# Five shared rows of wo: four of them moved from the partitions of DMA engine 3 to those of engines 2 and 4

## The chip, the cores and the metric

The kernel runs on one core of one Trainium2 chip. The metric is the device time of one launch in microseconds (us), as a median over several runs. Lower is better.

## What is computed

One decode step: an attention block over a cache, mixed by a gate with a small dense block. Cut to what matters:

```python
g = sigmoid((x * gate_w).sum(-1))                    # x: 1 x 1 x 512
q = (x @ wq) in 32 heads of 128                      # wq: 512 x 4096
scores = q . k_cache * 128 ** -0.5                   # 32 heads, 4096 keys of 128
o = softmax(scores) . v_cache                        # 32 heads, 4096 values of 128
a = o.reshape(4096) @ wo                             # wo: 4096 x 512
b = relu(x @ w1 + b1) ** 2 @ w2 + b2                 # w1: 512 x 1376, w2: 1376 x 512
out = g * a + (1 - g) * b                            # 1 x 1 x 512, all bf16
```

The two caches are 32 MB each, so the launch has 78.3 MB to read and very little arithmetic for each byte.

## The kernel before, in words

**Loads.** SP's queue issues, in a fixed order, four parts of `wq`, then `K0` to `K6`, then `V0`, `K7`, `V1`, `K8` and so on up to `V31` (`LAG` is 7). Each of these is one transfer of 128 partitions by 8 KB into a ring of 8 buffers (`Kt`, `Vt`). A load of K waits until VectorE and TensorE are done with the buffer (`s_sd`, `s_t`), one of V until its product is done (`s_pv`). `w1` and a first part of `w2` come after `K15` and `K17`; the rest of `w2` (`w2b`, `w2a`) and the last eight heads' part of `wo` (`wob_sb`, in `Kt`'s buffer 0) come at the very end, behind `V31`.

**Work on a head.** VectorE multiplies half of the keys by the head's q (L635), TensorE transposes the other half (L436) and multiplies (L447); ScalarE takes the exponentials; TensorE multiplies by V (`pv`, L472). Behind the last head come the sums with `wo` (L516, L535, L544), `w2` (L553), a transpose and the store.

**wo of the first 24 heads.** These 96 x 128 rows of `wo` are seen as 96 long rows of 32 KB (`woa_v`), and each long row goes into one partition of the tile `W`, where `wq` stood until its last use. Only 96 of the 128 partitions are needed, and the kernel chooses them:

[...]
- `RUNS`: 76 long rows, issued by POOL's queue at L327 (with small dummy transfers at L324 that turn the queue's round robin to the wanted engine), so that each row is carried by the engine that serves its partition. `FIRST`: 15 long rows in five transfers by SP's queue at L279, three rows each, on engines 0, 1 and 2. Counted from the two lists, engine 3 carries no whole row; engines 4, 5, 6 and 9 to 14 carry 5 each; engines 1 and 2 carry 7; engines 0, 7, 8 and 15 carry 8.
- `REST`: the last five long rows, in the list that the change touches. Each is cut into 16 parts of 2 KB, and each part into 1984 and 64 bytes, so that all 16 engines carry one sixteenth of it (L285). All of these parts land in one partition. They are issued with `V20`/`K27`, `V21`/`K28`, up to `V24`/`K31`, one row each time, and stand behind that K in the queue.

**Use of the rows.** `STRIPS` lists all the placements. POOL builds a selection matrix `selA` from it (L342, one instruction for each entry), by which `spread_a` puts each head's output on the partition that holds its row; partitions without a row get zeros. TensorE multiplies the first 23 columns (`out_a`, L516), VectorE the last nine (`part_y`, L682 and L685), and both wait for all of the rows (`s_wp`, `s_wr`).

Of the kernel before, what the change touches and what calls it, by code (L numbers as in the profile page):

```python
# [5 lines left out]
def bass_gated_mix__gqa_block_cached__dense_activation_squared_relu__decode_kernel(  # L6
# [57 lines left out]
            (SEAM, 7, 2, 3, 1), (WRAP, 15, 2, 3, 1)]  # L64
    FIRST = [(INNER, 0, 3, 0, 1), (INNER, 0, 3, 1, 1), (INNER, 0, 3, 2, 1), (INNER, 0, 3, 3, 1),
             (OUTER, 0, 3, 0, 1)]
    REST = [12, 13, 14, 15, 44]
    HF = 20

    def place(kind, e, k, r, m):  # L70
        if kind == INNER:
            return 32 + 4 * e + r, 4 // m, k * m
        if kind == OUTER:
            return (4 * e if e < 8 else 64 + 4 * e) + r, 4, k
        if kind == SEAM:
            return 28 + r, 68, k
        return r, 124, k
# [9 lines left out]
    def strips():  # L87
        q = 0
        for run in RUNS + FIRST:
            yield (*place(*run), q)  # L90
            q += place(*run)[2]
        for n, p in enumerate(REST):
            yield p, 1, 1, q + n
# [12 lines left out]
    with ctx:  # L106
# [147 lines left out]
        def _(eng):  # L254
# [16 lines left out]
            for h in range(NH):  # L271
# [5 lines left out]
                if HF <= h < HF + len(FIRST):  # L277
                    p, st, k, q = STRIPS[len(RUNS) + h - HF]
                    eng.dma_start(W[p:p + st * (k - 1) + 1:st, :], woa_v[q:q + k, :],  # L279
                                  max_dma_last_dim=8192).then_inc(s_wr, 16)  # L280
                if HF <= h < HF + len(REST):
                    p, _, _, q = STRIPS[len(RUNS) + len(FIRST) + h - HF]
# [113 lines left out]
        def _(eng):  # L396
# [111 lines left out]
            def out_a(n):  # L508
                if n == 0:
                    eng.wait_ge(s_ac, 2)  # L510
                    for q in s_wp:
                        eng.wait_ge(q, 16)
                    eng.wait_ge(s_wr, 16 * (len(FIRST) + 2 * len(REST)))
                for t in range(4 * n, min(4 * n + 4, TD)):
# [87 lines left out]
        def _(eng):  # L602
# [85 lines left out]
            for i in range(NH + LAG):  # L688
# [17 lines left out]
                if i == 33:  # L706
# [4 lines left out]
                    for q in s_wp:  # L711
                        eng.wait_ge(q, 16)
                    eng.wait_ge(s_wr, 16 * (len(FIRST) + 2 * len(REST)))
                    eng.wait_ge(s_y2, 1)
# [39 lines left out]
```

## Time and profile before

| | |
|---|---|
| median of 3 runs | 202.44 us (202.22 to 202.49) |
| profiled execution, its own time | 202.31 us |
| its span, first to last instruction | 200.5 us |
| DMA moved in the span | 78.76 MB, mean 393 GB/s |
| VectorE, TensorE, ScalarE busy | 69%, 67%, 40% of the span |
| K loads: 32 of 1024 KB, issue to landing | median 26.7 us |
| V loads: 32 of 1024 KB, issue to landing | median 27.4 us |

The page cuts the span into 40 slices of 5 us and gives the busy share in tenths. Beside what the page sums up, the trace holds each DMA packet (queue, start, duration, size) and each moment at which a load's semaphore was raised. A K or V load raises its semaphore 16 times, once for each DMA engine; the engine is not named, but the 16 moments of a load in order of time show how far apart the engines stand. The load is usable at the sixteenth.

### The profile page before, as it was taken

Reading aid. Unit: us, or ns where it says so; the run is one execution under the profiler, and the core shown is the slowest. Engines: PE = TensorE matmul, PEld = TensorE weight load, DVE = VectorE, ACT = ScalarE, POOL = GpSimd, SP = SyncE. Lnnn points to the kernel's source line nnn. Section 1 sums busy time; section 2 is a strip of 40 time slices with the busy share of each in tenths; the row PEclk is TensorE's granted clock in tenths of the full one; section 3 lists DMA queues with packets and bytes.
Section 4 is the critical chain, followed back from the end, with each engine's and each line's share of the span. In section 5 each row is a group of like instructions: output and inputs, shape, how many; then the busy total and the mean of one; then the engine's idle time right before and its main releaser. Section 6 shows DMA issues by size and latency. Waiting matters only on the chain.

```text
span 200.5 us, 6579 instructions
## 1 busy us (share of the span) xinstructions
PE 134.5 (67%) x2405; PEld 119.6 (60%) x2405; DVE 138.9 (69%) x1151; ACT 79.5 (40%) x148; POOL 30.6 (15%) x56
## 2 busy tenths in 40 slices
PE   0138657598986867646297763469997753598485
PEld 0106636387776667446276763459987653588484
DVE  0307999999998687447477774476699985577701
ACT  2105847376473336413147331433274330632000
POOL 2000000000000000000019930000398740000000
PEclk9999966655555555555555555555555555555555
DMA  6999999999999999999999999999999999999940
GB/s 236 426 425 425 418 420 422 415 418 425 409 415 425 420 414 411 419 419 419 418 425 417 412 418 407 410 407 415 413 406 401 402 393 415 374 425 415 372 173 10
DMA packets 12962, 78.76 MB, mean 393 GB/s; under 512 B 2658, under 2 KB 2836, under 8 KB 3861
## 3 DMA queue, kind: packets, MB, share of 16 engines
q1 hardware_dynamic: 11459, 75.83, 92.5%
q0 software_dynamic: 1456, 2.50, 3.3%
q8 instruction: 19, 0.31, 0.6%
q14 instruction: 14, 0.11, 0.2%
q10 hardware_dynamic: 14, 0.01, 0.0%
HBM read 78.32 MB, written 0.00 MB: 391 GB/s over the span
## 4 chain that ended last, share of the span: by engine, by line
DMA 59%; DVE 16%; SPq 12%; PE 9%; issue 2%; ACT 0%; DVEq 0%
DMA Kt<-in_A_k_cache_dram 41%; DVE Kt L635 14%; DMA Vt<-in_A_v_cache_dram 13%; DMA W<-in_A_wq_dram 5%; SPq L262 4%; SPq L267 3%; SPq L285 3%; PE KP L436 2%; PE pQ L414 2%; PE pQ L472 1%; DVE S L635 1%; SPq L279 1%; PE pO L472 1%; PE pX L544 1%; PE pS L447 1%
## 5 line engine op out<-in xcount | busy, mean ns | idle before, releaser
L635 DVE CUSTOM_DVE_ANT_0 Kt<-Kt,qb 128x128 bf16<-128x128 bf16 x512 | 113.4, 290 | 30.2 <-DMA Kt<-in_A_k_cache_dram 30.2
L370 ACT ACTIVATE kT<-KP 128x1024 bf16<-128x1024 bf16 x64 | 61.9, 1021 | 74.6 <-PE KP L436 74.6
L436 PE MATMUL KP<-ident,Kt 128*128 128x128 bf16 x512 | 57.1, 300 | 38.5 <-DMA Kt<-in_A_k_cache_dram 38.5
L436 PEld LDWEIGHTS KP<-ident,Kt 128*128 128x128 bf16 x512 | 49.6, 140 | 41.2 <-DMA Kt<-in_A_k_cache_dram 40.1
L635 DVE DVE_READ_ACCUMULATOR2_ANT S<- 128x1 f32 x512 | 41.3, 81 | 0.0
L447 PE MATMUL pS<-qcol,kT 128*128 128x1 bf16 x512 | 19.3, 167 | 8.3 <-DVE S L641 8.3
L447 PEld LDWEIGHTS pS<-qcol,kT 128*128 128x128 bf16 x512 | 19.0, 108 | 9.7 <-DVE S L641 9.7
L324 POOL DMA_DIRECT2D xb<-in_B_w_dram x9 | 5.4, 599 | 102.7 <-PE pQ L414 102.7
L414 PE MATMUL pQ<-W,xb 128*128 128x512 bf16 x32 | 15.0, 624 | 6.5 <-DMA W<-in_A_wq_dram 6.5
L472 PEld LDWEIGHTS pO<-E,Vt 128*128 128x128 bf16 x512 | 15.6, 105 | 1.2 <-issue 0.8
L472 PE MATMUL pO<-E,Vt 128*128 128x1 bf16 x512 | 16.2, 166 | 0.0
L342 POOL TENSOR_SCALAR_AFFINE_SELECT w_sb<-w_sb 24x36 bf16<-24x36 bf16 (+6 forms) x23 | 12.1, 527 | 3.7 <-POOL w_sb L342 0.5
L362 ACT ACTIVATE qb<-pQ 128x512 bf16<-128x512 f32 x8 | 4.7, 592 | 15.4 <-PE pQ L414 15.4
L414 PEld LDWEIGHTS pQ<-W,xb 128*128 128x128 bf16 x32 | 3.6, 130 | 11.0 <-issue 11.0
L472 PE MATMUL pQ<-E,Vt 128*128 128x1 bf16 x256 | 8.1, 165 | 3.0 <-DMA Vt<-in_A_v_cache_dram 2.4
L381 ACT ACTIVATE E<-S,nM 128x32 bf16<-128x32 f32 x32 | 9.9, 310 | 0.3
L472 PEld LDWEIGHTS pQ<-E,Vt 128*128 128x128 bf16 x256 | 7.7, 104 | 3.3 <-issue 3.2
L472 PEld LDWEIGHTS pX<-E,Vt 128*128 128x128 bf16 x256 | 7.9, 105 | 0.7 <-issue 0.6
L472 PE MATMUL pX<-E,Vt 128*128 128x1 bf16 x256 | 8.1, 166 | 0.0
L327 POOL DMA_DIRECT2D W<-in_A_wo_dram x13 | 7.3, 566 | 0.0
L621 DVE CAST qcol<-pQ 128x4 bf16<-128x4 f32 x8 | 1.2, 154 | 8.6 <-PE pQ L422 8.6
L641 DVE COPY S<-pS 128x16 f32<-128x16 f32 x32 | 5.4, 169 | 2.2 <-PE pS L447 2.2
(83 smaller groups left out, 90.9 us busy)
## 6 DMA issues: line engine op xcount, KB each, us to landing
Kt<-in_A_k_cache_dram SPq DMA_DIRECT2D x32, 1024.0 KB, 26.7
Vt<-in_A_v_cache_dram SPq DMA_DIRECT2D x32, 1024.0 KB, 27.4
W<-in_A_wq_dram SPq DMA_DIRECT2D x4, 1024.0 KB, 7.9
W<-in_A_wo_dram POOLq DMA_DIRECT2D x2, 768.0 KB, 13.0
w_sb<-in_B_w_dram SPq DMA_DIRECT2D x4, 344.0 KB, 22.8
w2a<-in_B_w_dram SPq DMA_DIRECT2D x1, 896.0 KB, 21.2
Kt<-in_A_wo_dram SPq DMA_DIRECT2D x1, 768.0 KB, 22.7
W<-in_A_wo_dram POOLq DMA_DIRECT2D x9, 64.0 KB, 23.4
```

The lines of the kernel that those rows point to most:

```text
L262: eng.dma_start(Kt[:, h % NK, :], k_h[h, :, :]).then_inc(s_k[h % NK], 16)
L267: eng.dma_start(Vt[:, h % NV, :], v_h[h, :, :]).then_inc(s_v[h % NV], 16)
L285: eng.dma_start(to[:, :, x:y], of[:, :, x:y]).then_inc(s_wr, 16)
L327: eng.dma_start(W[p:p + st * (k - 1) + 1:st, :], woa_v[q:q + k, :], max_dma_last_dim=8192).then_inc(s_wp[n], 16)
L342: eng.affine_select(out=part, in_=part, compare_op=ALU.not_equal, fill=1.0, base=-st * q, pattern=[[st, 4], [-1, st * (k - 1) + 1]], chann ...
L370: eng.activation(kT[:, h % 2, j * HB * 128:(j + 1) * HB * 128], KP[n % 3][:, :], ACT.Copy).then_inc(s_ev, 1)
L381: eng.activation(E[:, h % NE, :], S[:, h % NS, :], ACT.Exp, bias=nM[:, h:h + 1], scale=SCALE, accum_out=RS[:, h:h + 1]).then_inc(s_e, 1)
L414: mm = eng.matmul(pQ[:, :], xb[:, t, :], wq_sb[:, t, c * 512:(c + 1) * 512], start=(t == 0), stop=(t == 3))
L436: mm = eng.transpose(KP[n % 3][:, y * 128:(y + 1) * 128], Kt[:, h % NK, b * 128:(b + 1) * 128], ident[:, :])
L447: mm = eng.matmul(S2[:, y:y + 1], kT[:, h % 2, y * 128:(y + 1) * 128], qcol[:, h:h + 1], start=True, stop=True)
L472: mm = eng.matmul(O(h, h + 1), Vt[:, h % NV, b * 128:(b + 1) * 128], E[:, h % NE, b:b + 1], start=(b == 0), stop=(b == NB - 1))
L635: ins = eng.tensor_tensor_reduce(kb, kb, qb[:, h * 128:(h + 1) * 128], 1.0, 0.0, ALU.mult, ALU.add, S[:, h % NS, b:b + 1])
```

## The change

Four of the five shared rows go into other partitions. [...] The rows keep their order, so the first shared row goes to engine 2's partition, the second, third and fourth to engine 4's, the fifth stays. Transfers, sizes, queues and waits are the same ones; POOL's selections write other columns of the same matrix.

```diff
-    REST = [12, 13, 14, 15, 44]
+    REST = [11, 17, 18, 19, 44]
```

## The prediction

> **What bounds the kernel now.** I read the page's slices and queues first, then the chain that ended last, then SP's timeline, then the trace's records of packets and semaphores.
>
> ```profile
> DMA  6999999999999999999999999999999999999940
> q1 hardware_dynamic: 11459, 75.83, 92.5%
> q0 software_dynamic: 1456, 2.50, 3.3%
> q8 instruction: 19, 0.31, 0.6%
> DMA 59%; DVE 16%; SPq 12%; PE 9%; issue 2%; ACT 0%; DVEq 0%
> ```
>
> The DMA engines are busy from the second slice to 190 us, while no compute engine is over 69%. So the launch lasts as long as the slowest DMA engine, plus a tail. The chain's last entries, in order of time, show the tail:
>
> ```profile
> 165.81 25.49 DMA Vt<-in_A_v_cache_dram
> 191.31 0.14 issue
> 191.44 0.99 PE pQ L472 x32
> 192.43 1.71 PE pX L544 x8
> 194.14 0.32 PE pX L516 x12
> 194.46 0.87 PE pQ L472 x32
> 195.42 0.24 DVE onorm L662
> 196.85 0.41 PE pX L553 x12
> 197.26 0.88 PE pX L535 x32
> 198.69 0.21 DVE fin L725
> ```
>
> `V30` lands at 191.30 and from there TensorE runs without a wait: product 30, two sums with `wo`, product 31, the last sums, end. `V31` landed at 193.77, 0.7 before it was needed; the two last parts of `wo` at 196.82 and 197.46, 0.3 us and less ahead. So the end follows the landings of `V30` and `V31` one for one.
>
> SP's timeline shows that nothing is starved of work:
>
> ```profile
> 151.15 2.27 SPq L285 DMA_DIRECT2D W<-in_A_wo_dram  x2
> 153.46 19.63 SPq L267 DMA_DIRECT2D Vt<-in_A_v_cache_dram  x7
> 174.08 2.81 SPq L298 DMA_DIRECT2D Kt<-in_A_wo_dram  x2
> ```
>
> All is issued by 177 us, 20 us before the last landing: what is late is late on a DMA engine.
>
> **Which engine.** The 16 moments at which a load's semaphore rises, from the trace (us; first, fifteenth, last engine):
>
> ```
> V14   107.49  109.66  113.72     before POOL's rows of wo
> K27   142.94  150.36  150.82     after them
> K30   163.04  166.46  168.95
> V25   171.02  174.62  177.61     after the shared rows
> V31   186.24  190.43  193.77
> ```
>
> One engine is 4.06 us behind the fifteenth at `V14`. The 76 rows on POOL's queue bring the others back to it (0.46 at `K27`). That is what the lists say of engine 3, the only one without whole rows. Then, while the shared rows run, one engine falls 3 us behind once more, and stays 3.34 behind to `V31`. Is it engine 3 again, and do the shared rows do it? Two things in the packet records say yes.
>
> First, an engine's packets follow each other by 3 to 4 ns of overlap, so one engine can be traced from end to start. A packet of 8192 bytes takes 309 to 321 ns nearly everywhere. The engine whose part of the first shared row starts at 148.26 has in the next 5.6 us packets of 538, 475, 389, 386, 395, 396 and 475 ns, then 538, 398, 367, 431, 469 and so on, one after another, as the others' parts come by. Its part of the last row starts at 174.47, the last of the sixteen (the one before it at 171.59). So the engine that is stretched is the one that ends last, and all five rows have in common that they land in partitions of engine 3.
>
> Second, where many parts come at once, all engines stand: after 10 parts begun between 154.47 and 154.89 nearly every packet takes 340 to 495 ns, and after 12 between 170.11 and 170.51 up to 830 ns.
>
> **What a shared row costs.** The traced engine needs 174.47 - 148.26 = 26.21 us from its first part to its last, that is four rounds of one V, one K and one part. Another, followed in the same way through parts at 154.60, 159.87, 165.23 and 170.28, needs 15.68 for three, 5.23 each. So the traced one loses 26.21 - 4 x 5.23 = 5.3 us against it. One stretch of 0.62 (packets of 764 and 475 ns, 455 and 166 over) falls on an instruction fetch of queue 8 at 149.95, which leaves 4.7, or 0.9 to 1.2 a row, by whether one counts five rows or the four rounds. I take 1.0. The others lose by the common stalls: 0.05, 0.21, 0.31, none seen, and 0.56 us for rows one to five.
>
> [...]
>
> **The change, part by part.** Instructions, transfers and bytes are the same ones; the ten DMAs of L285 and POOL's 23 selections of L342 change their addresses only, so they cost nothing more (POOL ends at 164.0, and the matrix is read at 181.4; if that cover of 17 us were gone, each selection would count 0.5). What moves is which engine is slowed:
>
> - **Engine 3** is rid of rows one to four. Of the 4.7 it keeps row five, whose stretch beyond the common stall is 0.5 (packets of 399, 1052 and 551 ns, 1.07 over, less 0.56). It gains 4.2 by that count; by 0.8 of the 4.7, 3.8; by nothing if its lag had another source; less than nothing has no reason, as no work comes to it. I take 3.9, so its `V31` lands at 193.77 - 3.9 = 189.9.
> - **Engine 4** takes rows two to four. Where does it stand? It is one of nine engines with five whole rows, and at `V31` nine moments lie together, 188.52 to 189.02, with five between 189.45 and 190.43 (there I look for engines with eight rows) and one at 186.24. I take 188.8. Three rows at 1.0 make 3.0, less 0.2 for stalls that it has already in part: 2.8, so 191.6. The bounds are 2.0 (rows at 0.9, stalls of 0.5 and 0.2 off) and 3.7 (three rows at 1.24, what 32 KB cost an engine that carries them alone: four packets of 0.31).
> - **Engine 2** takes row one: 1.0, from at most 190.43, so 191.4 at the latest. It is level with engine 4 and doesn't move the end.
> - **The common stalls** stay: the parts of the pack still come together to one partition. Bounds: none of the 1.1 us left, or 0.56 for each of five rows, 2.8, that is 1.7 more.
>
> So the last landing of `V31` goes from 193.77 to 191.6, 2.2 us earlier, and `V30` with it. The next in line then is TensorE's own tail: product 29, done 1.75 us after its V lands and followed by 0.8 of sums, fits the interval of 2.5 to `V30`. L544 waits for VectorE's `part_y`, which ended at 189.23 and would be needed at about 190.1; it starts behind work on the last heads that comes earlier too. So the 2.2 is kept: span 200.5 - 2.2 = 198.3, the profiled execution's 202.31 - 2.2 = 200.1, and as it stands 0.13 under the median, 200.2.
>
> [...] The stretched packets above decide for the owner of the partitions; no row names an engine by number.
>
> **The rivals.**
>
> - **The lag changes hands.** Engine 4 is not among the nine but at 190.43, and pays 3.4 to 3.7: `V31` at 193.8 to 194.1. Time 202.4 to 202.8, mostly no change. For it: the records don't name engines. Against: the count of nine.
> - **Slower, by the pack's stalls.** Engine 4 runs with the pack, engine 3 ran beside it. If parts sent into the partitions of an engine in step stall all sixteen at each row as row five did (1.7 us more), and engine 4 pays 3.7 above that, it ends at 188.8 + 1.7 + 3.7 = 194.2: 202.9. It decides from 5.4 us on engine 4 in all: 5.0 to be level with 193.77, 0.4 to be seen. For it: the stall grows from 0.05 to 0.56 as the parts draw together. Against: row four brought 8 parts within 0.4 us and no common stall.
> - **Nothing to do with the partition.** Fetches and semaphores made the lag, as up to `V14`, where no shared row ran. Then engine 3 stays at 193.77: 202.4, no change. Against: the stretched packets, seen in none of the slices before 140 us.
> - **More than I count.** Engine 4 pays 2.0 or less and engine 2 is the one at 186.24: the end falls to the fifteenth's 190.43, 3.3 us earlier: 199.1.
>
> **How the numbers follow.** The forecast with its bounds (engine 4 at 190.8 to 192.7, time 199.5 to 201.4) has 0.68, the larger gain 0.14, the lag that changes hands 0.06, nothing to do with the partition 0.04, slower 0.08. About 0.2% (0.4 us) is what a measurement of this kernel can tell from no change; faster by more than that has 0.68 + 0.14 + half of the handed lag, 0.85; within it 0.04 and a third of that lag, 0.06; slower 0.08 and the rest of it, 0.09. The range 199.0 to 201.8 takes in the larger gain and leaves out the three last cases, 0.18.
>
> **What would show it.** In the changed profile `V31`'s last moment lies near 191.6 and the last but one near 191; the gap between them is about 1 us or less instead of 3.34. Product 31 (the last L472) starts near 192.2, not 194.46. Parts of row one to four no longer go with a chain of stretched packets on an engine that is last at row five. If the last engine is still 3 us behind, I was wrong on whose lag it is; if the gap is closed but the whole pack is later, wrong on the stalls.

## The result, and the profile after

The changed kernel takes 198.98 us (median of five runs, 198.77 to 199.34) against 202.29 on the same occasion before (202.20 to 202.49): a ratio of 0.9837, 95% interval 0.9822 to 0.9851. That is 3.3 us faster; 2.2 were forecast, and the result lies 0.02 us under the lower end of the range. The profiled execution took 198.77 with a span of 197.0, 3.5 less than before.

The page's rows after, in the order in which those of before were shown (busy tenths of the DMA engines; queue, packets, MB and share; the chain that ended last by engine):

```profile
DMA  6999999999999999999999999999999999999991
q1 hardware_dynamic: 11459, 75.83, 94.1%
q0 software_dynamic: 1456, 2.50, 3.4%
q8 instruction: 19, 0.31, 0.6%
DMA 72%; DVE 17%; PE 7%; issue 2%; SPq 1%; ACT 0%; DVEq 0%
```

The packets and bytes are the same ones to the last digit. The engines' shares rise by as much as the span falls, so no DMA work has gone: there is less time in which fifteen engines have finished and one has not (at `V31` 3.34 us before and 0.36 after, in the moments below).

The last entries of the chain, in order of time (start, us, what):

```profile
170.28 20.14 DMA Vt<-in_A_v_cache_dram
190.42 0.14 issue
190.56 1.01 PE pQ L472 x32
191.57 0.03 issue
...
191.66 0.24 DVE onorm L662
...
192.69 0.52 PE pS L526 x16
193.21 0.42 PE pX L553 x12
193.63 0.99 PE pX L535 x32
...
195.16 0.21 DVE fin L725
```

The chain now runs through `V31`, which lands at 190.42, and TensorE waits for it; before, it ran through `V30`. From `V31`'s landing to the end of the span it was 200.5 - 193.77 = 6.7 us and is 197.0 - 190.42 = 6.6, so the end moved about as far as the landing.

What holds these 6.6 us together is a second wait, which this chain does not show. The sum of L535 needs the first part of `wob_sb`, which comes behind `V31` on the same DMA engines. Its last landing, from the trace's semaphores, and the start of L535 in TensorE's timeline (us):

```
             V31     first part of wob_sb   L535 starts   end of span
before       193.77  196.82                 197.12        200.51
after        190.42  193.44                 193.58        196.98
```

The part lands 3.05 and 3.02 us behind `V31`. After the change L535 starts 0.14 behind this landing, and so it does, to 0.01, when the kernel is run again and in n_none, n_e4, d2, f_e1 and f_spread below. In these seven profiles L535 starts 0.43 to 0.63 behind the start of the L553 before it; in the other six, where its load landed 0.20 to 0.56 earlier, 0.34. So in the seven TensorE waits for the load, by 0.1 to 0.3 us, and the end belongs to the DMA engines still, but to a load that comes behind `V31`. In d2's profile the chain itself runs that way:

```profile
171.58 22.71 DMA Kt<-in_A_wo_dram
194.30 0.14 issue
194.44 1.00 PE pX L535 x32
```

SP's timeline after (start, us, what):

```profile
150.72 2.26 SPq L285 DMA_DIRECT2D W<-in_A_wo_dram  x2
153.02 17.59 SPq L267 DMA_DIRECT2D Vt<-in_A_v_cache_dram  x7
171.60 2.01 SPq L298 DMA_DIRECT2D Kt<-in_A_wo_dram  x2
```

The last shared row is issued 0.4 us earlier than before, and what comes behind the last V 2.5 us earlier (171.60, not 174.08), because each V waits for a product that waits for the slowest engine.

The 16 moments at which a load's semaphore rises, from the trace's records (us; first, second, eighth, fifteenth, last):

```
        before                                    after
K27     142.94 143.87 148.51 150.36 150.82        143.04 144.15 148.54 150.32 150.44
V27     176.26 176.88 178.81 179.60 182.57        176.85 177.94 178.47 179.22 179.44
V31     186.25 188.52 188.95 190.43 193.77        187.87 188.09 188.66 190.06 190.42
```

The gap between the fifteenth and the last at `V31` went from 3.34 to 0.36 us. What was not forecast stands at the other end: the engine that was early by 2.3 us in `V31` is no longer early. No engine has come out as a new last one.

### The profile page after: what moved, and what is told of

The parts are those of the page before. It is cut to its first block, busy times and chain, and to the rows that moved or that the text cites. A ratio compares the mean times of both kernels' runs of the same rounds, so it can differ in the third digit from the quotient of the medians.

```text
span 197.0 us, 6573 instructions
## 1 busy us (share of the span) xinstructions
PE 129.9 (66%) x2399; PEld 116.8 (59%) x2405; DVE 138.8 (70%) x1151; ACT 79.4 (40%) x148; POOL 30.5 (15%) x56
## 4 chain that ended last, share of the span: by engine, by line
DMA 72%; DVE 17%; PE 7%; issue 2%; SPq 1%; ACT 0%; DVEq 0%
DMA Kt<-in_A_k_cache_dram 56%; DVE Kt L635 15%; DMA Vt<-in_A_v_cache_dram 10%; DMA W<-in_A_wq_dram 6%; PE KP L436 2%; PE pO L472 1%; DVE S L635 1%; PE pQ L414 1%; SPq L256 1%; PE pM L461 1%; PE pQ L472 1%; PE pX L535 1%; PE pS L447 0%; PE pX L553 0%; ACT qb L362 0%
## 5 line engine op out<-in xcount | busy, mean ns | idle before, releaser
L436 PE MATMUL KP<-ident,Kt 128*128 128x128 bf16 x512 | 54.4, 291 | 37.3 <-DMA Kt<-in_A_k_cache_dram 37.3
L436 PEld LDWEIGHTS KP<-ident,Kt 128*128 128x128 bf16 x512 | 47.3, 135 | 40.0 <-DMA Kt<-in_A_k_cache_dram 38.9
L414 PE MATMUL pQ<-W,xb 128*128 128x512 bf16 x26 | 12.5, 626 | 7.9 <-DMA W<-in_A_wq_dram 6.5
L327 POOL DMA_DIRECT2D W<-in_A_wo_dram x13 | 7.3, 564 | 0.0
```

The source lines that it names most:

```text
L414: mm = eng.matmul(pQ[:, :], xb[:, t, :], wq_sb[:, t, c * 512:(c + 1) * 512], start=(t == 0), stop=(t == 3))
L436: mm = eng.transpose(KP[n % 3][:, y * 128:(y + 1) * 128], Kt[:, h % NK, b * 128:(b + 1) * 128], ident[:, :])
```

## The experiments

Two theories for what was slow: **A**, parts that land in a partition slow the engine that serves it, by a price for each row; **B**, engine 3 is late for another reason (instruction fetches, semaphores). And for the size of the gain: **A1**, engine 4 pays that price and had the room for it; **A2**, engine 4 had no room and the price is small. `V27` is the best load to compare the runs in, since all the shared rows are past and the moments are least spread there.

### Without rows, and with three rows on one engine

The four kernels of this set leave shared rows out, so a part of the attention's output is missing. Behind each `#` stands the run.

```diff
-    REST = [11, 17, 18, 19, 44]
+    REST = [None, None, None, None, None]   # n_none
+    REST = [None, 12, 13, 14, None]         # n_e3
+    REST = [None, 17, 18, 19, None]         # n_e4
+    REST = [None, 101, 102, 103, None]      # n_e9
...
-                if HF <= h < HF + len(REST):
-                    p, _, _, q = STRIPS[len(RUNS) + len(FIRST) + h - HF]
+                if HF <= h < HF + len(REST) and REST[h - HF] is not None:
+                    p, q = REST[h - HF], Q0 + h - HF
```

`Q0` is 91, the first shared row; `strips` skips the empty entries and the waits count the rows that are left.

> Leaves out the five shared rows (their part of the output is missing). Theory A, the rows that land in a partition slow the engine that serves it: without rows no engine is alone behind, the gap between the fifteenth and the last moment of V31 is under 0.6 us, and every engine is rid of its own parts (0.5) and of the common stalls (about 1), so the last moment of V31 lies at 188.5 to 189.5. Theory B, fetches or semaphores made engine 3 late: the last moment stays about 3 us behind the fifteenth.

> Only shared rows two to four, into partitions 12, 13 and 14 of engine 3 (the first and the last row are left out). Theory A at 1.0 a row: against the run without rows one moment of V31 moves by 2.5 to 3.5 us, beyond what all 16 share. Theory B: none does.

> Only shared rows two to four, into partitions 17, 18 and 19 of engine 4 (the first and the last row are left out). Theory A1, every owner pays about 1.0 a row and engine 4 was the early engine (186.24 at V31 before): against the run without rows one early moment of V31 moves by about 2.8 us and the last one hardly. Theory A2, engine 4 was one of the nine and pays 0.5 a row or less: one moment in the middle moves by 1.5 us or less. My prediction (one of the nine, 1.0 a row): one moment becomes the last, 1 us or more behind the fifteenth.

> Only shared rows two to four, into partitions 101, 102 and 103 of engine 9 (the first and the last row are left out). Theory A1: engine 9 stands elsewhere than engine 4 and pays the same 2.8 us; if it is one of the nine, its moment becomes the last of V31, 1 us or more behind the fifteenth. Theory A2: no moment moves by more than 1.5 us beyond what all share.

One execution of each: 197.71, 199.36, 198.38 and 200.57 us, beside 202.67 for the kernel before. `V27`'s moments from the trace:

```
          first  second third  4th    eighth 15th   last
n_none    174.96 175.91 176.68 177.08 177.22 177.90 178.16
n_e3      175.42 176.38 177.46 177.59 177.72 178.66 179.71
n_e4      176.59 177.53 177.84 177.90 178.06 178.67 178.88
n_e9      175.83 176.87 177.55 178.10 178.21 178.77 181.45
```

**n_none** decides against B: without rows no engine is behind at `V27` (0.26 us), and at `V31` the last moment is 189.32 with a gap of 0.59. Of the packets of 8192 bytes on SP's queue that began between 142 and 175 us, 7 took over 330 ns, where 156 did in the kernel before.

**n_e9** shows that the price is not engine 3's or engine 4's alone. All other moments are 0.9 later than in n_none; one is alone behind, at 181.45. Where it stood without rows is between 177.08 and 178.16, so it paid 2.4 to 3.5 us for three rows beyond what all paid: 0.8 to 1.2 a row.

**n_e3** does the same to engine 3. The third moment, 176.68, is the one that is missing from the row (0.47 later it would be 177.15), and 179.71 has come: 2.6 us beyond the common shift, 0.85 a row.

**n_e4** is the run that explains the size. The common shift is again 0.7 to 0.9: 175.91 goes to 176.59 and 176.68 to 177.53. The first moment, 174.96, has gone into the pack, to 177.84 at the least, 2.0 or more beyond the common shift and 3.1 at most. In the other three runs the earliest moment stays. At `V31` it is the same: the first moment of n_none, 184.90, is gone, and the first of n_e4 is 187.79. So engine 4 *is* the early engine, paid the price, and had room for nearly all of it: A1. My own place for it, one of a group of nine, would have made it last by 1 us or more; the gap in `V31` is 0.67.

The numbers 3, 4 and 9 are the kernel's names for these engines; no record holds a number. What the three runs show is that rows in partitions 12 to 14, in 17 to 19 and in 101 to 103 each delay one moment of the sixteen, and a different one each time: the third of n_none (176.68), the first (174.96), and one between 177.08 and 178.16. That 15 and 44 go with 12 to 14 rests on the one chain of stretched packets that was followed from the first shared row to the last in the trace of before. For partition 11, and for 7, 21, 25 and 105 in the runs that follow, no run shows by itself which engine it belongs to.

### How many rows engine 3 carries, and other owners

```diff
-    REST = [11, 17, 18, 19, 44]
+    REST = [12, 13, 18, 19, 44]             # d3_three_on_e3
+    REST = [12, 17, 18, 19, 44]             # d2_two_on_e3
+    REST = [11, 17, 18, 19, 7]              # f_e1_none_on_e3
+    REST = [17, 21, 25, 101, 105]           # f_spread_five_owners
```

> All five shared rows, three of them in engine 3's partitions (12, 13, 44) and two in engine 4's (18, 19). Theory A with a floor: engine 3's last moment of V31 is 193.77 with five rows and falls by 1.1 a row, the others end at 190.4; so 191.6 here, time 200.1 (199.7 to 200.6). Theory C, engine 3 pays only while it is the last one, so that the price is not by the row: the time is that of one row (199.0) or that of five (202.3).

> All five shared rows, two in engine 3's partitions (12, 44) and three in engine 4's. Theory A with a floor: engine 3 comes to 190.5, level with the rest: time 199.0 to 199.5, the same as the changed kernel or up to 0.5 above it. Theory C: 199.0 or 202.3.

> All five shared rows, none on engine 3: the fifth goes to partition 7 of engine 1. Theory A with a floor: engine 3 was not the last any more, so freeing it brings nothing; engine 1 carries seven rows and may come to stand behind the rest by up to 1.1: time 198.8 to 200.0. If engine 3 with one row was still the last: 198.5.

> All five shared rows, one each in the partitions of engines 4, 5, 6, 9 and 10. Theory A with a floor: each owner pays about 1.1, but four of the five stand in the pack without room, so the last moment of V31 goes up by 0.3 to 1.1 and the time is 199.3 to 200.1, worse than three rows on the one engine that had room. If spreading as such were what helped, 198.5 to 199.0.

Medians, and the ratio to the kernel before with its interval (the changed kernel was run again in the next set, beside 202.32 for the kernel before):

```
rows on engine 3                       us       ratio   95%              last of V27   last of V31
5  kernel before                       202.24                            182.57        193.77
3  d3_three_on_e3                      200.88   0.9935  0.992 - 0.995    181.06        192.35
2  d2_two_on_e3                        199.65   0.9873  0.9858 - 0.9888  180.16        191.20
1  the changed kernel, again           198.97   0.9838  0.9822 - 0.9855  179.38        190.59
0  f_e1_none_on_e3                     199.19   0.985   0.9835 - 0.9865  179.74        190.87
0  f_spread_five_owners                199.67   0.9885  0.9863 - 0.9906  179.38        190.25
```

The price goes by the row, with a floor: d3's 200.88 lies between the two times that theory C allows, and C is out. From five rows to three the last moment of `V27` falls by 0.75 a row, less than the 1.1 that I expected, and d3 came out 0.3 above its range. With two rows engine 3 is in the pack (a gap of 0.18 at `V27`), and there the pack itself is some 0.7 later than after the change, which put d2 0.15 above its range. From one row to none nothing is gained: the last engine is another by then. d3 also bounds engine 4's price from below. Its first two moments at `V27` are 176.95 and 178.24, in the kernel before 176.26 and 176.88. If 176.95 is the second engine, which has no rows in either, engine 4 went from 176.26 to 178.24 or beyond by two rows, 1.0 a row at the least, while the eighth moment is 0.07 earlier.

**f_spread** has a time inside its range and a mechanism outside it. I expected the last landing of `V31` to go up by 0.3 to 1.1; it is at 190.25, no later than after the change. One row more fits there as it stands: in n_none the fourth to the twelfth moment of `V27` lie 0.8 to 1.1 ahead of the last. Which engines these are is not shown. The time came from behind `V31`. The chain, in order of time:

```profile
184.33 0.14 issue
184.47 0.35 PE pQ L472 x8
184.82 1.81 issue
186.63 0.78 PE pQ L472 x24
...
189.12 1.71 PE pX L544 x8
190.82 0.32 PE pX L516 x12
191.14 0.87 PE pQ L472 x32
...
192.65 0.63 issue
...
194.45 0.08 issue
194.53 1.01 PE pX L535 x32
```

Product 29 stops after eight matmuls for 1.81 us, which the profile books under "issue": the profile shows nothing that TensorE waits for. The same stop in TensorE's timeline after the change (start, us, engine, line, what, and the idle time before it in brackets):

```profile
184.95 0.35 PE L472 MATMUL pQ<-E,Vt 128*128 128x1 bf16 x8 [1.47 <-DMA Vt<-in_A_v_cache_dram]
185.78 0.78 PE L472 MATMUL pQ<-E,Vt 128*128 128x1 bf16 x24 [0.48 <-issue]
```

Eleven of the thirteen profiles show such a stop, 0.21 to 1.81 us long, and in each a 16 KB instruction packet of queue 8 ends 1.2 to 1.5 us before TensorE goes on (183.41 + 1.14 = 184.55 after the change; 184.07 + 1.13 = 185.20 in f_spread). That the stop is a wait for code, as the expectation for the second run of the changed kernel calls it, fits this, but no run here takes the fetch away, so it is not shown. With it, `V31` had been there for 0.9 us when product 31 began.

Yet these stops did not set the end. The first part of `wob_sb` lands at 194.39, 4.1 us behind `V31` where all other runs have 3.0 to 3.3, and L535 starts 0.14 after it; TensorE alone would have been there 0.2 earlier. At that landing one engine is 1.05 us behind the fifteenth (193.34), where it was 0.41 behind at `V31`. Why it fell back there is open.

### Whole rows instead of shared ones

If engines 2 and 4 have the room, they might as well carry whole rows and spare the others their parts. POOL's list gets the rows, the shared list loses them:

```diff
-            (SEAM, 7, 2, 3, 1), (WRAP, 15, 2, 3, 1)]
+            (SEAM, 7, 2, 3, 1), (WRAP, 15, 2, 3, 1),
+            (OUTER, 2, 1, 3, 1), (OUTER, 4, 1, 1, 1), (OUTER, 4, 1, 2, 1)]   # g1
+            (OUTER, 2, 1, 3, 1), (OUTER, 4, 3, 1, 1), (OUTER, 4, 1, 2, 1)]   # g2
...
-    REST = [11, 17, 18, 19, 44]
+    REST = [19, 44]                                                          # g1
+    REST = []                                                                # g2
```

> The changed kernel once more, beside the next two on the same chip. 198.8 to 199.2. If TensorE's code wait in product 29 (0.48 us in the profile of after) is much the same, the span ends 6.6 us after the last moment of V31.

> Three of the five rows carried whole by POOL's queue: one by engine 2 into partition 11, two by engine 4 into 17 and 18; two stay shared (19 of engine 4, 44 of engine 3). If engines 2 and 4 have the room that the changed kernel gave to shared rows, a whole row costs them 1.24 instead of about 0.9, and all sixteen are rid of three parts each (0.3) and of some of the common stalls: 198.2 to 198.8. If the room was not there, engine 4 (two whole rows, one shared: 3.4) is the last: 199.2 or more.

> All five rows carried whole: one by engine 2, two by engine 4, one each by engines 5 and 6; nothing shared. No parts and no common stalls, so the bound is the run without rows (197.7) if engines 5 and 6 have room for 1.24, and 198.5 to 199.2 if they stand at the end of the pack.

The changed kernel again: 198.97 us (0.9822 to 0.9855 of before). g1: 199.30 (0.9827 to 0.987). g2: 199.01 (0.982 to 0.985). Neither is faster than the change. g1's time lies where I expected it if engine 4 had no room, but its `V31` landed at 190.40, no later than in the changed kernel (190.59). In g2 the landing of `V31` did come earlier, 189.65, and that of the first part of `wob_sb` too, 192.96 against 193.61, and the tail took a part of it back:

```profile
184.09 0.33 PE pQ L473 x7
184.42 1.04 issue
185.46 0.80 PE pQ L473 x25
...
190.00 0.87 PE pQ L473 x32
...
191.20 0.82 issue
192.02 0.28 PE KP L523
```

Two stops, 1.04 and 0.82 us, that the profile books under "issue" lie on the way; the span ends 7.2 us after `V31`'s last landing, where it was 6.6 after the change. The stop of 1.04 is gone through before `V31` is there, and 190.00 is 0.35 after the landing. Of the stop of 0.82 about 0.3 counts: the last sum (here L536) starts at 193.44 in TensorE's timeline, and 0.14 behind its load would have been 193.10. g1 was 198.75 to 199.66 in its four runs, too spread to say more than that it is no better.

## Why the prediction was right or wrong, point by point

- **What bounds the kernel: right, with the tail less simple than told.** Span less the last landing of `V31` is 6.5 to 6.7 in before, after, n_none, n_e3, n_e4, d3, d2 and f_e1. In the changed kernel the last wait is for the first part of `wob_sb`, 3.0 to 3.1 behind `V31` in all of these, on the same engines. The difference is 7.1 in n_e9, where TensorE, after a stop of 1.3 us in product 29, comes to product 31 later than `V31` lands, and 7.6 in f_spread, where that part of `wob_sb` is late.
- **Which engine, and why: right.** The engine that ended last was the owner of the rows' partitions, and the rows did it: no lag without them (n_none, a gap of 0.26 us at `V27`), a lag of another engine when they lie in partitions 101 to 103 (n_e9, 2.68). The rival that the partition had nothing to do with it is out: moving four rows off engine 3's partitions brought the gap at `V31` from 3.34 us to 0.36.
- **The price of a row: about right.** 1.0 was taken; 0.85 on engine 3, 0.8 to 1.2 on engine 9, 1.0 or more on engine 4 (d3), 0.75 between five rows and three were measured. Engine 2's one row is in no run by itself.
- **Engine 4's place: wrong, and this is the step that failed.** I put it among "nine engines with five whole rows" because nine moments of `V31` lay together, at 188.8. The records name no engine, and the count that fitted was chance: engine 4 was the single one at 186.25, 2.55 us earlier. I even had that moment in the working and gave it, in the rival "more than I count", to engine 2. The trace of before held a warning: at `V27` two engines, not one, stood 2.4 and 1.8 us ahead of the third (178.66), so the groups of `V31` were not lasting ones. The lists' counts themselves are borne out: in the trace of before, the 16 moments of POOL's last transfer of rows (L327) stand in groups of 1, 2, 1, 9 and 3 (135.83; 137.03 and 137.34; 138.56; 140.78 to 142.60; 144.22 to 144.69), as the engines do that have 0, 2, 3, 5 and 8 rows in `RUNS`. Why engine 4 was ahead at `V31`, with five whole rows like eight others, no run shows. With the right place the same sum reads 186.25 + 2.8 = 189.05 for engine 4, which is then not the last one; the last is the fifteenth of before at 190.43, 3.34 us earlier than 193.77, and 202.44 - 3.34 = 199.1. Measured: 190.42 (190.59 in the second profile) and 198.98. The mechanism was right, and the term for engine 4 was 2.55 us too high. The 199.1 of that rival came true, but not for its reason: engine 4 paid 2.0 to 3.1 for three rows (n_e4), but from an earlier place.
- **Engine 3's gain, 3.9 of the 4.7: not contradicted.** It need only come to 190.42 or before, 3.35 of gain, and it did.
- **Common stalls: they stay, as said.** Packets of 8192 bytes over 330 ns between 142 and 175 us: 156 before, 176 after. What they and the parts themselves cost is seen in n_none, whose `V31` lands 1.1 us before that of the change.
- **The lag changes hands: out.** The last engine at `V31` is 0.36 us behind the fifteenth. No run shows the 3.4 us that this rival took as the lower price of three rows on engine 4: in n_e4 they cost 2.0 to 3.1.
- **The slower rival: out.** The pack's eighth moment at `V27` is 0.34 us earlier than before, not later, though rows two to four now go to an engine that moves with the pack once it has lost its lead. Two counts in the working were off: 8 parts of 1984 bytes, not 10, begin between 154.47 and 154.89, and 11, not 12, between 170.11 and 170.51. So row four, with 8 parts and no stall, was no argument against this rival: rows two and three had 8 parts as well, and behind each of the two more than a dozen packets took over 400 ns.

## What to carry to other kernels

Here all sixteen DMA engines were busy to 190 us, and the time was that of the last engine: its `V31` came 3.35 us earlier and the span ended 3.5 earlier. The 16 semaphore moments of one load showed how much room each of the others had (engine 4: 2.0 us at least). A transfer that many engines write into one partition was paid by the engine that serves the partition, 0.75 to 1.2 us a row, so it was best placed on the one with room. But such moments carry no names: before a sum is built on where a named engine stands, move something that only that engine feels and see which moment goes, as three rows did here. And once the last engine was level with the rest, what had been hidden behind it began to count: a stop in the tail (0.3 us in g2), or a smaller load behind the last large one (4.1 us behind `V31` in f_spread, 3.0 after the change).

## What the runs showed of the hardware that was not expected

- A row of 32 KB written by 16 engines into one partition cost the owner about as much as carrying most of it: 0.75 to 1.2 us, where four packets of 8192 bytes at 0.31 make 1.24. The owner paid it though it carried only a sixteenth of the row itself.
- Such rows stretched the packets of engines that write elsewhere, too. Add up, over all engines, what each packet of 8192 bytes begun between 142 and 175 us took above 312 ns: it is 7.0 us in n_none, 14 to 20 with three rows, and 21 to 33 with five. The owner's own price, 2.6 us for three rows in n_e3, is only a part of that.
- TensorE's stop in the middle of product 29 lasted 0.48 us after the change and 1.81 in f_spread, with the same instructions on TensorE; it ended 1.2 us after an instruction packet in the one and 1.4 in the other.
